# A fixed first expert for the second line of slots in a fused attention and two-layer mixture-of-experts kernel

## The chip, the cores and the metric

One core of one Trainium2 chip. The number that counts is device microseconds of one launch, the median of several runs.

## What is computed

Attention with a window (half of the heads plain, half dilated), then two mixture-of-experts layers of eight experts each. Every token goes to the one expert with the largest logit.

```python
x = attn_out.transpose(0, 2, 1, 3).reshape(2304, 512)
for layer in (1, 2):
    e_idx = argmax(x @ w_gate [+ modality_bias[modality_id] in layer 2], axis=1)
    for e in range(8):
        mask = e_idx == e
        h = maximum(x[mask] @ w1[e], 0)           # w1[e]: 512 x 1024
        out[mask] = gate[mask] * (h @ w2[e])      # w2[e]: 1024 x 512; layer 1 has one more sigmoid factor
    x = out
```

## The kernel before

The program is one long hand-ordered stream on each engine: attention (16 head pairs, function names st...), then `moe` for layer 1, then `moe` for layer 2. Instruction order on an engine is program order; a step that is to run in the middle of another one is hung on a **hook**, `(s, k)`: slot `s`, place `k` inside the slot. The tables `plan` near the end of the program (`at(s, k, ...)`) say what hangs where.

**Slots.** A slot is one block of up to 128 tokens of one expert: 96 matmuls `ph<-xT,wb` (`mm1`, two groups of 48 that fill `ph0` and `ph1`), ReLU and split of the result into a high and a low half (`hsplit`: `hh` on ScalarE, `hl` on VectorE), 24 matmuls `py<-wb` (`hh` first, then `hl`). Numbers are kept as pairs of float16 (high and low), so weights arrive as float32 in the buffer `raw` (8 pieces of 1024 columns, 512 KB each; one buffer for all experts), are rounded on ScalarE (`hi_piece`, L100, letter H in the lists) and their remainder is formed on VectorE (`lo_piece`, L105, letter L; B is both; D sends the next expert's pieces into the part of `raw` that has come free).

**Two lines of slots.** Slots 0 to 2 work on one early expert `g`, found from the first four token tiles in `first_expert`, whose weights are sent during attention. From slot 3 on, even slots walk through the first half of the list of blocks and odd slots through the second half (the list begins with expert `g` and goes round); each line has its own split weight buffer (`wb0`, `wb1`), so that one line can change its expert while the other computes. The cut is at `h`, half of the number of blocks. Which expert the odd line begins with is therefore known only after the **sort** of all tokens.

**The sort** (`sort`, a generator that runs in pieces: `run(so1)`) turns all 2304 logits into the list of token numbers of each slot. Its pieces hang at (0,0), (0,1), (0,5), (0,10), (1,3) and (2,2). The piece at (0,1) counts the blocks (`nb`, `nall`, `h`), makes the block number of each slot (`bs`, `bm`, on GpSimd, L746 to L749), then on VectorE the token positions (`ps`, `pos`, `pi`, L753 to L767) and two one-hot arrays (`ob`, `obp`, L804 and L805). The piece at (0,10) issues the gathers of tokens for slots 2 to 4, runs `table()` on VectorE (expert of each slot, where weights change) and sends slot 3's weights by that table (`start.weights(KE, always=True)`, a register loaded by SyncE from the table). The piece at (1,3) works out the gate factors on VectorE (`dl` to `gate`, L829 to L843) and GpSimd: six small operations (`gr`, `g3`, L847 to L852) and four products `Bg` (L855). The piece at (2,2) sums them on TensorE (`pg<-Bga,Aa`, L862) between the two groups of slot 2's `mm1`.

Slot 3's weights are split by `first_splits` at (1,5), (1,6), (2,0) and (2,3) of the plan (lists `FIRST`), which also sends slot 4's weights behind them. At (1,6) and (2,1) the gathered tokens of slots 2 and 3 are transposed (`x_turned`: TensorE `pxt`, then a copy on ScalarE, L901). The results of slots 0 and 1 go out at (2,5) and (2,6) (`Post1.out`, rows `y` to `y_dram`); nine spare rows of `y_dram` are filled with zeros (`zero`, on SyncE's queue).

Of the kernel before, what the change touches and what calls it, by code (L numbers as in the profile page):

```python
# [53 lines left out]
def fused(ctx, tc, qk, vw, wr1, w1a, w2a, mid, wr2, mbias, w1b, w2b, cf, c16, cbs, cms, cib, out, dbg=None):  # L54
# [646 lines left out]
    def sort(nm, lg, nt, inv, fe, ea, tab, scale, og, extra, gscale, start):  # L701
# [67 lines left out]
        def table():  # L769
# [8 lines left out]
            v.tensor_tensor(hn, nall, h, op=ALU.subtract)
            v.tensor_scalar(lim, s_odd, hn, hm, op0=ALU.mult, op1=ALU.add)
            sc = T("sc", [NSLOT])  # L780
            v.scalar_tensor_tensor(out=sc, in0=bs, scalar=-float(KA), in1=lim, op0=ALU.add, op1=ALU.min)
# [588 lines left out]
```

## Time and profile before

| what | value |
|---|---|
| median of 3 runs | 647.51 us (646.09 to 647.54) |
| the profiled execution: its own time | 648.77 us |
| its span, first to last instruction | 647.0 us |
| TensorE matmul busy | 593.6 us (92%), 7425 instructions |
| VectorE busy | 363.9 us (56%) |
| ScalarE busy | 273.0 us (42%) |
| GpSimd busy | 198.2 us (31%) |
| mean granted TensorE clock | 0.967 of full speed |

The profiled execution took 1.26 us more than the median of the runs, and 1.77 us of its time lie outside its span. Attention fills the first 152 us of the span, layer 1 goes from there to about 428 us, layer 2 to the end. Slot 0 begins at 152.3 us, slot 1 at 167.4, slot 2 at 181.1, slot 3 at 194.6, slot 4 at 209.9; later slots take 11.3 us each.

In the answers of the trace a line is: start in us, duration in us, engine, line of the program, operation, what is written and read, number of instructions merged (x), and in brackets the idle time just before and what ended it.

### The profile page before, as it was taken

The numbers are of one execution on the slowest core, as the hardware profiler recorded it, in microseconds if no ns is written. First come the engines' busy times: TensorE is split into PE (matmuls) and PEld (weight loads), VectorE is DVE, ScalarE is ACT, GpSimd is POOL, SyncE is SP. The second block draws the span as 40 slices with busy tenths as digits, with TensorE's granted clock in tenths as the row PEclk, the third lists the DMA queues.
The fourth block names the chain that finished last, engine by engine and source line by source line (L and its number), as shares of the span: only waits on it lengthen the run. The fifth ranks groups of instructions, "written<-read, shape, count | busy, mean of one in ns | idle before, by whom it ended". The sixth has DMA issues, their size and how long they took to land. (4 is left out here: it accounts for less than half of the span.)

```text
span 647.0 us, 19443 instructions
## 1 busy us (share of the span) xinstructions
PE 593.6 (92%) x7425; PEld 459.1 (71%) x7425; DVE 363.9 (56%) x643; ACT 273.0 (42%) x370; POOL 198.2 (31%) x315
## 2 busy tenths in 40 slices
PE   3989889968988999999999899989999999999994
PEld 2878778867665767777686686867686767777772
DVE  6798898898777436953848922248541111013460
ACT  5667767773184114923626511111532111114550
POOL 2567767613271310101110410001554212222220
PEclk9789989976999999999999999989999999999998
DMA  8765768972499854994877763310985534143921
GB/s 285 241 190 187 216 186 273 287 161 71 153 360 293 231 131 135 308 348 120 237 227 216 223 143 58 56 31 7 312 304 140 125 51 100 50 100 96 305 62 37
DMA packets 100865, 114.17 MB, mean 176 GB/s; under 512 B 64399, under 2 KB 69263, under 8 KB 100752
## 3 DMA queue, kind: packets, MB, share of 16 engines
q1 hardware_dynamic: 95072, 94.89, 51.3%
q0 software_dynamic: 5280, 17.13, 8.4%
q8 instruction: 60, 0.98, 0.6%
q10 hardware_dynamic: 400, 0.72, 0.3%
q14 instruction: 53, 0.43, 0.2%
HBM read 209.13 MB, written 18.22 MB: 351 GB/s over the span
## 5 line engine op out<-in xcount | busy, mean ns | idle before, releaser
L922 PEld LDWEIGHTS <-wb 128*128 128x128 f16 x4032 | 230.7, 99 | 10.1 <-issue 5.1
L922 PE MATMUL ph<-xT,wb 128*128 128x128 f16 x3648 | 211.1, 219 | 3.2 <-ACT xT L901 2.7
L933 DVE SCALAR_TENSOR_TENSOR hl<-ph,hh 128x512 f16<-128x512 f32 x84 | 57.8, 690 | 164.6 <-ACTq L941 153.5
L996 PE MATMUL py<-wb,hh 128*128 128x512 f16 x608 | 137.8, 379 | 1.7 <-ACT hh L932 1.7
L105 DVE SCALAR_TENSOR_TENSOR wb<-raw,wb 128x1024 f16<-128x1024 f32 (+1 forms) x80 | 104.9, 1350 | 16.5 <-ACT wb L100 14.3
L996 PEld LDWEIGHTS <-hh 128*128 128x128 f16 x672 | 63.6, 98 | 71.0 <-ACT hh L932 2.7
L932 ACT ACTIVATE hh<-ph 128x512 f16<-128x512 f32 x84 | 50.2, 598 | 148.9 <-PE ph L922 140.7
L100 ACT ACTIVATE wb<-raw 128x1024 f16<-128x1024 f32 (+1 forms) x80 | 87.4, 1136 | 10.5 <-DMA raw<-in_w1a 3.1
L996 PE MATMUL py<-wb,hl 128*128 128x512 f16 x304 | 71.8, 379 | 0.0
L996 PEld LDWEIGHTS <-hl 128*128 128x128 f16 x336 | 32.8, 98 | 40.0 <-DVE hl L933 0.6
L1261 POOL DMA_INDIRECT out<-y,idx x16 | 16.2, 1011 | 97.5 <-ACTq L941 78.4
L447 PE MATMUL po<-v,pT 128*96 128x65 f32 x384 | 41.6, 262 | 0.0
L447 PEld LDWEIGHTS po<-v,pT 128*96 128x96 f32 x384 | 38.4, 177 | 0.0
L386 PE MATMUL ps<-kk,qs 128*96 128x128 f16 x192 | 30.0, 229 | 4.3 <-DVE kk L344 2.2
L386 PE MATMUL ps<-kk,ql 128*96 128x128 f16 x192 | 30.1, 230 | 3.8 <-DVE ql L364 3.8
L434 ACT ACTIVATE pT<-pst 128x384 f32<-128x384 f32 x48 | 23.5, 490 | 23.0 <-PE pst L433 22.4
L387 DVE TENSOR_REDUCE M<-ps 96x4 f32<-96x512 f32 x48 | 31.6, 680 | 2.8 <-PE ps L386 2.3
L885 POOL DMA_INDIRECT xg<-x_dram,idxaa x23 | 24.4, 1063 | 27.5 <-DMA xT<-xg 15.4
L1260 ACT ACTIVATE y<-py,gsb 128x512 f32<-128x512 f32 x16 | 11.0, 687 | 51.8 <-PE py L996 51.8
L431 PE MATMUL pst<-mt,msel 128*128 128x96 bf16 x192 | 30.5, 218 | 2.4 <-ACT mt L420 2.4
L386 PEld LDWEIGHTS <-ql 128*96 128x96 f16 x192 | 23.6, 130 | 12.4 <-DVE ql L364 5.4
L433 PE MATMUL pst<-ql,kk 128*128 128x96 f16 x192 | 30.6, 219 | 0.0
(405 smaller groups left out, 730.4 us busy)
## 6 DMA issues: line engine op xcount, KB each, us to landing
raw<-in_w1a SPq DMA_DIRECT2D x95, 512.0 KB
raw<-in_w2a SPq DMA_DIRECT2D x92, 512.0 KB
raw<-in_w1b SPq DMA_DIRECT2D x75, 512.0 KB
raw<-in_w2b SPq DMA_DIRECT2D x72, 512.0 KB
qk<-in_qk SPq DMA_DIRECT2D x16, 608.0 KB
v<-in_vw SPq DMA_DIRECT2D x16, 390.0 KB
y_dram<-y SPq DMA_DIRECT2D x11, 260.0 KB
y_dram<-lotmp SPq DMA_DIRECT2D x10, 260.0 KB
```

The lines of the kernel that those rows point to most:

```text
L100: nc.scalar.activation(wb[:, 0, s], raw[:, s], AF.Copy, scale=SW)
L105: nc.vector.scalar_tensor_tensor(out=wb[:, 1, s], in0=raw[:, s], scalar=SW, in1=wb[:, 0, s], op0=ALU.mult, op1=ALU.subtract)
L386: nc.tensor.matmul(ps[:, j, :], q[:, h, QT * i:QT * i + QT], kk[:, h, QT * i:QT * i + 128], start=False, stop=w == 1 and j == 3, skip_grou ...
L387: nc.vector.tensor_reduce(out=Ms[n][:, 4 * g:4 * g + 4], in_=ps, axis=AX.X, op=ALU.max)
L431: nc.tensor.matmul(ps[:, j, :], msel[:, typ, j, :], mt[:, g, :], start=j == 0, stop=False, skip_group_check=True)
L433: nc.tensor.matmul(ps[:, j, :], kk[:, h, QT * i:QT * i + 128], q[:, h, QT * i:QT * i + QT], start=False, stop=w == 1 and j == 3, skip_grou ...
L447: nc.tensor.matmul(po[:, h, i, :], pT[:, NQ * h + i, :], v[:, h, i, :], start=True, stop=True)
L885: nc.gpsimd.indirect_dma_start(t, None, src, bass.IndirectOffsetOnAxis(start.idx[:, s:s + 1], 0))
L922: nc.tensor.matmul(ph[:, j, :], w[:, c, fs], xT[:, parts[c + i], :], start=k == 0, stop=k == 47, skip_group_check=True)
L932: nc.scalar.activation(hs, ph, AF.Relu)
L933: nc.vector.scalar_tensor_tensor(out=hl[:, 4 * g:4 * g + 4, :], in0=ph, scalar=0.0, in1=hs, op0=ALU.max, op1=ALU.subtract)
L996: nc.tensor.matmul(to, a, w, start=k == 0, stop=k == len(ops) - 1)
```

## The change

The odd line begins with the expert four places on from `g`, `(g + 4) mod 8`. `first_expert` works out that number (`gj`) and a mark of the first four experts of the list (`low`). The sort no longer cuts the list at `h` but between the fourth and the fifth expert: `a4` blocks lie before the cut, `b4` behind it; the line that runs out first takes the last blocks of the other. The weights of slot 3 are sent by `second`, in two parts, with a register loaded from `gj`: pieces 0 to 5 at (0,0), pieces 6 and 7 where the table's send was. Their split is spread over (0,5), (1,0), (1,5), (1,6), (2,0) and (2,2). Layer 2 keeps the old way.

```diff
 def slot_consts():
+        v.tensor_tensor(s_line, s_odd, s_half, op=ALU.mult)
+        v.tensor_scalar(s_line, s_line, -1.0, None, op0=ALU.add)
...
 def first_expert(nm, lg0, psum, fe):
+        if nm == "a":
+            g4, gj, low, q0 = T("g4", [P, 1]), T("gj", [P, 1], I32), T("low", [P, E]), T("q0", [P, E])
+            gp.tensor_scalar(g4, g, 4.0, -8.0, op0=ALU.is_ge, op1=ALU.mult)
+            gp.tensor_tensor(g4, g4, g, op=ALU.add)
+            gp.tensor_scalar(gj, g4, 4.0, None, op0=ALU.add)
+            gp.tensor_scalar(low, o, 4.0, None, op0=ALU.is_lt)
+            gp.tensor_scalar(q0, o, 4.0, None, op0=ALU.is_equal)
+            fe.update(gj=gj, low=low, q0=q0)
...
 def sort(...):
-        gp.tensor_scalar(bs, s_odd, h, None, op0=ALU.mult)
-        gp.tensor_tensor(bs, bs, s_half, op=ALU.add)
-        gp.tensor_scalar(bm, s_even, h, 1000.0, op0=ALU.is_ge, op1=ALU.mult)
-        gp.tensor_tensor(bm, bm, bs, op=ALU.add)
+        if start.fixed:
+            v.tensor_tensor(e8, nb, fe["low"], op=ALU.mult)
+            v.tensor_reduce(out=a4, in_=e8, axis=AX.X, op=ALU.add)
+            gp.tensor_tensor(hn, nall, h, op=ALU.subtract)
+            gp.tensor_scalar(bm, s_even, h, 1000.0, op0=ALU.is_ge, op1=ALU.mult)
+            gp.tensor_scalar(bt[:, 0], s_line, hn, 1000.0, op0=ALU.is_ge, op1=ALU.mult)
+            gp.tensor_tensor(bm, bm, bt[:, 0], op=ALU.add)
+            gp.tensor_tensor(bm, bm, s_half, op=ALU.add)
+            gp.tensor_tensor(b4, nall, a4, op=ALU.subtract)
+            v.scalar_tensor_tensor(out=bs, in0=s_odd, scalar=a4, in1=bm, op0=ALU.mult, op1=ALU.add)
+            v.tensor_scalar(bt[:, 0], s_even, a4, hn, op0=ALU.is_ge, op1=ALU.mult)
+            v.tensor_scalar(bt[:, 1], s_line, b4, hn, op0=ALU.is_ge, op1=ALU.mult)
+            v.tensor_tensor(bs, bs, bt[:, 0], op=ALU.add)
+            v.tensor_tensor(bm, bs, bt[:, 1], op=ALU.subtract)
...
         def table(...):     # three operations on VectorE become nine
...
         for i in range(KA, KA + 3):
             start.gather(i)
         table()
-        start.weights(KE, always=True)
+        if start.fixed:
+            start.second(6, 8)
+        else:
+            start.weights(KE, always=True)
...
+        def second(a, b):
+            if a == 0:
+                regs["second"] = nc.sync.value_load(fe1["gj"][0:1, 0:1], min_val=0, max_val=E - 1)
+            load_raw(w1, w2, regs["second"], pieces=range(a, b))
+            if b == 8:
+                regs.pop("second")
...
-    at(0, 0, run(so1), lambda: lo_piece(wbuf[0], 12))
+    at(0, 0, run(so1), lambda: lo_piece(wbuf[0], 12), lambda: start1.second(0, 6))
     at(0, 1, run(so1, 2))
     at(0, 2, run(fss))
-    at(0, 5, run(so1), lambda: lo_piece(wbuf[0], 14))
+    at(0, 5, run(so1), lambda: lo_piece(wbuf[0], 14), sp1("H0:4 H4:8"))
     at(0, 10, run(so1, 2))
+    at(1, 0, sp1("H8:12 L0:2"))
     at(1, 3, run(so1), start1.consts)
-    at(1, 5, lambda: start1.first_splits(FIRST[0]))
-    at(1, 6, lambda: start1.turned(KA), lambda: start1.first_splits(FIRST[1]))
-    at(2, 0, lambda: gt.memset(y16p[1][:, 2 * DM:], 0.0), lambda: start1.first_splits(FIRST[2]))
+    at(1, 5, sp1("L2:6 D0:6 H12:16"))
+    at(1, 6, lambda: start1.turned(KA), sp1("L6:10 D6:10"))
+    at(2, 0, lambda: gt.memset(y16p[1][:, 2 * DM:], 0.0), sp1("L10:12 D10:12"))
     at(2, 1, lambda: start1.turned(KA + 1))
-    at(2, 2, run(so1))
-    at(2, 3, lambda: start1.first_splits(FIRST[3]))
+    at(2, 2, run(so1), sp1("L12:16 D12:16"))
```

How this moves instructions, at the places where the order matters. TensorE's own order stays word for word the same. (Lines are those of each program; the changed one is longer, so `hl`, L933, is L976 there.)

VectorE in slot 0, behind the count of the cut (`ha`), before:

```order
L744 TENSOR_REDUCE ha<-hsa 128x1
L753 TENSOR_TENSOR e2a<-fe_Msa,nba 128x64
L754 TENSOR_REDUCE basea<-e2a 128x8
L756 SCALAR_TENSOR_TENSOR psa<-rk,basea 128x144
L757 TENSOR_TENSOR psa<-psa,oha 128x144
```

VectorE at the same place with the change:

```order
L756 TENSOR_REDUCE ha<-hsa 128x1
L760 TENSOR_TENSOR e8a<-nba,fe_lowa 128x8
L761 TENSOR_REDUCE a4a<-e8a 128x1
L768 SCALAR_TENSOR_TENSOR bsa<-slots_77,a4a,bma 128x27
L769 TENSOR_SCALAR bta<-slots_77,a4a,hna 128x27
L770 TENSOR_SCALAR bta<-slots_77,b4a,hna 128x27
L771 TENSOR_TENSOR bsa<-bsa,bta 128x27
L772 TENSOR_TENSOR bma<-bsa,bta 128x27
L781 TENSOR_TENSOR e2a<-fe_Msa,nba 128x64
L782 TENSOR_REDUCE basea<-e2a 128x8
```

Seven operations stand in front of the position arithmetic, and the third of them reads `bma`, which GpSimd writes. On GpSimd the four operations on `bs` and `bm` have become six:

```order
L762 TENSOR_TENSOR hna<-nalla,ha 128x1
L763 TENSOR_SCALAR bma<-slots_77,ha 128x27
L764 TENSOR_SCALAR bta<-slots_77,hna 128x27
L765 TENSOR_TENSOR bma<-bma,bta 128x27
L766 TENSOR_TENSOR bma<-bma,slots_77 128x27
L767 TENSOR_TENSOR b4a<-nalla,a4a 128x1
```

Behind these, `ob`, `obp`, the two `hl` of slot 0 and the array `A` follow on VectorE as before.

VectorE from the gate factors of the sort (end of slot 1) into slot 2, before:

```order
L843 RECIPROCAL gatea<-dena 128x18
L1097 SCALAR_TENSOR_TENSOR wr2h<-wr2t,wr2h 128x32
L933 SCALAR_TENSOR_TENSOR hl<-ph_3061,hh 128x512
L105 SCALAR_TENSOR_TENSOR wb_2654<-raw,wb_2654 128x2048 x3
L933 SCALAR_TENSOR_TENSOR hl<-ph_3179,hh 128x512
L105 SCALAR_TENSOR_TENSOR wb_2654<-raw,wb_2654 128x2048
L933 SCALAR_TENSOR_TENSOR hl<-ph_3296,hh 128x512
```

and with the change:

```order
L886 RECIPROCAL gatea<-dena 128x18
L1147 SCALAR_TENSOR_TENSOR wr2h<-wr2t,wr2h 128x32
L976 SCALAR_TENSOR_TENSOR hl<-ph_3097,hh 128x512
L105 SCALAR_TENSOR_TENSOR wb_2666<-raw,wb_2666 128x2048 x2
L105 SCALAR_TENSOR_TENSOR wb_2666<-raw,wb_2666 128x1024
L105 SCALAR_TENSOR_TENSOR wb_2666<-raw,wb_2666 128x2048
L976 SCALAR_TENSOR_TENSOR hl<-ph_3213,hh 128x512
L976 SCALAR_TENSOR_TENSOR hl<-ph_3329,hh 128x512
```

All remainders of slot 3's weights (a first one of 1024 columns has moved up, behind `table()`) now stand ahead of both `hl` of slot 2. On ScalarE three of the four roundings (L100, 128x2048) of these weights moved ahead of slot 1's `hh`; one is left in front of the copy of slot 2's tokens.

SyncE's queue with the change, from the last stores of attention on:

```order
L496 DMA x_dram<-x_2464 96x1x512 x6
L92 ISA
L92 DMA raw<-in_w2a 128x2x512
L92 ISA
L92 DMA raw<-in_w2a 128x2x512
L1151 DMA y_dram<-zt 128x1040 x9
L92 ISA
L92 DMA raw<-in_w2a 128x2x512
L92 ISA
L92 DMA raw<-in_w2a 128x2x512
L953 TENSOR_LOAD tab_2687
```

Pieces 0 to 3 stand ahead of these rows, around the last transposing read of attention. The nine stores of zeros stood among attention's first loads before; now they stand between pieces 5 and 6. All eight pieces now stand ahead of the load of the table's register, which stood ahead of all eight before.

## Rows read from the trace of the kernel before

**Rows 1.** The page, part 5: the group of `hl` (two in each slot).

```profile
L933 DVE SCALAR_TENSOR_TENSOR hl<-ph,hh 128x512 f16<-128x512 f32 x84 | 57.8, 690 | 164.6 <-ACTq L941 153.5
```

**Rows 2.** TensorE's waits from 170 us to the end: total us, times, longest.

```profile
PE ph L922 <- ACT xT L901: 2.7, 2, 1.6
...
PE py L996 <- ACT hh L932: 1.7, 2, 1.2
...
PE pyt L1151 <- ACT y L1132: 0.7, 1, 0.7
PE pyt L1151 <- DVE y L1133: 0.4, 1, 0.4
```

**Rows 3.** ScalarE's timeline: first rounding of slot 3's weights; `y` of slot 2.

```profile
178.19 1.91 ACT L100 ACTIVATE wb<-raw 128x2048 f16<-128x2048 f32 x1 [3.12 <-DMA raw<-in_w1a]
...
200.33 0.69 ACT L1132 ACTIVATE y<-py,gsa 128x512 f16<-128x512 f32 x1 [8.04 <-DMA y_dram<-y]
```

**Rows 4.** VectorE's timeline, the sort in slot 0.

```profile
158.17 0.18 DVE L744 TENSOR_REDUCE ha<-hsa 128x1 f32<-128x27 f32 x1
158.27 0.21 DVE L753 TENSOR_TENSOR e2a<-fe_Msa,nba 128x64 f32<-128x64 f32 x1
...
161.94 1.28 DVE L933 SCALAR_TENSOR_TENSOR hl<-ph,hh 128x512 f16<-128x512 f32 x2
```

**Rows 5.** GpSimd's timeline, the sort in slot 0; operations of this size later.

```profile
158.46 0.39 POOL L746 TENSOR_SCALAR bsa<-slots,ha 128x27 f32<-128x27 f32 x1 [4.47 <-DVE ha L744]
...
188.22 0.30 POOL L868 TENSOR_SCALAR gsa<-gsa 128x27 f32<-128x27 f32 x1
188.50 0.24 POOL L870 TENSOR_SCALAR inva<-fla 128x27 f32<-128x27 f32 x1
```

**Rows 6.** TensorE's timeline, slots 0 to 2.

```profile
162.68 1.90 PE L996 MATMUL pya<-wb,hl 128*128 128x512 f16 x8 [0.16 <-DVE hl L933]
...
181.05 1.95 PE L922 MATMUL ph<-xT,wb 128*128 128x128 f16 x32 [1.65 <-ACT xT L901]
...
184.64 1.04 PE L862 MATMUL pg<-Bga,Aa 128*128 128x108 f16 x18
```

**Rows 7.** GpSimd's timeline, the gate factors.

```profile
175.71 0.30 POOL L847 TENSOR_SCALAR gra<-gatea 128x18 f32<-128x18 f32 x1 [4.84 <-DVE wr2h L1097]
...
177.37 2.92 POOL L855 TENSOR_TENSOR Bga<-oba,g3a 128x486 f16<-128x486 f16 x3
180.24 3.05 POOL L855 TENSOR_TENSOR Bga<-oba,midf 128x486 f16<-128x486 f16 x1
```

**Rows 8.** VectorE's timeline: slot 1's first `hl`; first remainder of slot 3's weights.

```profile
172.41 0.69 DVE L933 SCALAR_TENSOR_TENSOR hl<-ph,hh 128x512 f16<-128x512 f32 x1 [1.55 <-ACT hh L932]
...
180.13 2.30 DVE L105 SCALAR_TENSOR_TENSOR wb<-raw,wb 128x2048 f16<-128x2048 f32 x1 [3.89 <-ACT wb L100]
```

**Rows 9.** GpSimd and VectorE side by side in attention.

```profile
94.15 0.77 POOL L404 CAST mb<-r 96x12 bf16<-96x12 f32 x1
95.00 0.72 POOL L405 TENSOR_TENSOR r<-r,mb 96x12 f32<-96x12 f32 x1
...
94.07 0.79 DVE L344 SCALAR_TENSOR_TENSOR kk<-qk,kk 64x608 f16<-64x608 f32 x1
94.89 0.76 DVE L364 SCALAR_TENSOR_TENSOR ql<-qk,qs 64x576 f16<-64x576 f32 x1
```

**Rows 10.** Stretches: from:to and length, PE, PEld, DVE, ACT, POOL busy, PE clock, DMA.

```profile
427.20:430.60 3.40, 1.33 (x20) 0.83 (x19) 0.92 (x2) 0.69 (x1) 0.18 (x1) 0.95 0.03 10
430.60:434.00 3.40, 3.40 (x44) 3.20 (x45) 1.97 (x6) 0.00 (x0) 1.02 (x1) 0.55 0.20 78
...
178.00:181.40 3.40, 1.75 (x14) 0.88 (x13) 1.26 (x1) 3.21 (x3) 3.40 (x4) 1.00 1.04 399
```

**Rows 11.** SyncE's queue: first weights of slot 3, first result row.

```profile
171.48 1.78 SPq L92 DMA_DIRECT2D raw<-in_w1a  x4
...
192.91 0.43 SPq L1140 DMA_DIRECT2D y_dram<-y  x1
```

More of the change, by code (lines that the diff above doesn't have):

```diff
@@ L141, in fused @@
     midf = const.tile([P, NT], F32, name="midf")
-    slots4 = const.tile([P, 4, NSLOT], F32, name="slots4")
-    s_half, s_odd, s_even, s_two = (slots4[:, i] for i in range(4))
+    slots4 = const.tile([P, 5, NSLOT], F32, name="slots4")
+    s_half, s_odd, s_even, s_two, s_line = (slots4[:, i] for i in range(5))
     lg2 = const.tile([P, NSLOT, E], F32, name="lg2")
@@ L215, in first_expert @@
         v.tensor_scalar(own, desc, m, None, op0=ALU.is_equal)
+        if nm == "a":
+            v.tensor_tensor(own, own, fe["q0"], op=ALU.add)
         yield
@@ L745, in sort @@
         bs, bm = T("bs", [NSLOT]), T("bm", [NSLOT])
[L746 to L749 removed]
+        if start.fixed:
+            a4, b4, hn, e8, bt = T("a4", [1]), T("b4", [1]), T("hn", [1]), T("e8", [E]), T("bt", [2, NSLOT])
+            v.tensor_tensor(e8, nb, fe["low"], op=ALU.mult)
[12 more added lines that the diff above has]
+        else:
+            gp.tensor_scalar(bs, s_odd, h, None, op0=ALU.mult)
+            gp.tensor_tensor(bs, bs, s_half, op=ALU.add)
+            gp.tensor_scalar(bm, s_even, h, 1000.0, op0=ALU.is_ge, op1=ALU.mult)
+            gp.tensor_tensor(bm, bm, bs, op=ALU.add)
         nbb = nb.unsqueeze(1).to_broadcast([P, E, E])
@@ L767, in sort, with table @@
         v.tensor_scalar(pi[:, 2], pi[:, 0], 127, None, op0=ALU.bitwise_and)
-        def table():
+        def table(hn=hn if start.fixed else None):
             end = T("end", [E])
@@ L775, in table @@
             v.tensor_scalar(nlast, nall, KA - 1.0, None, op0=ALU.add)
-            hm, hn, lim = T("hm", [1]), T("hn", [1]), T("lim", [NSLOT])
+            hm, lim, sc = T("hm", [1]), T("lim", [NSLOT]), T("sc", [NSLOT])
             v.tensor_scalar(hm, h, -1.0, None, op0=ALU.add)
[L778 to L781, printed above, removed]
+            if start.fixed:
+                hq = T("hq", [1])
+                v.tensor_scalar(hq, hn, -1.0, None, op0=ALU.add)
+                v.tensor_scalar(bt[:, 0], s_even, hm, None, op0=ALU.min)
+                v.tensor_scalar(bt[:, 1], s_line, hq, None, op0=ALU.min)
+                v.tensor_tensor(sc, bt[:, 0], bt[:, 1], op=ALU.add)
+                v.scalar_tensor_tensor(out=sc, in0=s_odd, scalar=a4, in1=sc, op0=ALU.mult, op1=ALU.add)
+                v.tensor_scalar(lim, bt[:, 0], a4, hn, op0=ALU.is_ge, op1=ALU.mult)
+                v.scalar_tensor_tensor(out=sc, in0=sc, scalar=1.0, in1=lim, op0=ALU.add, op1=ALU.add)
+                v.tensor_scalar(lim, bt[:, 1], b4, hn, op0=ALU.is_ge, op1=ALU.mult)
+                v.tensor_tensor(sc, sc, lim, op=ALU.subtract)
+            else:
+                hn = T("hn", [1])
+                v.tensor_tensor(hn, nall, h, op=ALU.subtract)
+                v.tensor_scalar(lim, s_odd, hn, hm, op0=ALU.mult, op1=ALU.add)
+                v.scalar_tensor_tensor(out=sc, in0=bs, scalar=-float(KA), in1=lim, op0=ALU.add, op1=ALU.min)
             cmp2 = T("cmp2", [NSLOT, E])
@@ L824, in sort @@
         table()
-        start.weights(KE, always=True)
+        if start.fixed:
+            start.second(6, 8)
+        else:
+            start.weights(KE, always=True)
         yield
@@ L1008, in slot @@
             hook(7)
-        start.part = part
+        start.part, start.second = part, second
         start.gather, start.transpose, start.turned, start.weights, start.pys = gather, x_transpose, x_turned, weights, pys
@@ L1032, in fused @@
     class Start:
-        name, next, late_low = "a", NEXT, True
+        name, next, late_low, fixed = "a", NEXT, True, True
         def hook(self, s, k):
@@ L1224, in fused @@
     class Start2(Start):
-        name, next, late_low = "b", NEXT2, False
+        name, next, late_low, fixed = "b", NEXT2, False, False
         def fields(self, g, inv, ex):
```

2 lines of the change are left out of this document (added).

## The prediction

> **What bounds the kernel now.** I began with the waits of TensorE: from 170 us to the end only a few are left, and four of them lie where the change works [rows 2]. Slot 2 starts 1.65 us late, because the copy of its tokens stands on ScalarE behind the first rounding of slot 3's weights (178.19 to 180.10 us), and that one waited 3.12 us for its transfer [rows 3, 6]. In slot 3 TensorE waits 0.7, 0.4 and 1.7 us: `y` of slot 2 could be written only at 200.33 us, after 8.04 us in which ScalarE waited for the first result row to leave the same buffer, a store issued at 192.91 us; two roundings and then `hh` stood behind it [rows 2, 3, 11]. So what the table's late send costs on TensorE's path is at most 1.6 + 2.8 = 4.4 us. Everything that the change adds to the sort must be set against that, and the next views are therefore the timelines of VectorE and GpSimd in slots 0 to 2.
>
> The amount of work stays. I put the reference's inputs through the two routers: expert 2 is `g`; 256 of its tokens go to slots 0 and 1, and the remaining blocks of experts 0 to 7 are 4, 3, 1, 3, 2, 2, 3, 3, in sum 21. That makes 23 slots, 19 follow in layer 2 with either order, and the trace has 84 `hl`, two for each of 42 slots [rows 1]. Before, the cut `h` = 11 falls just between experts 6 and 7, so that the odd line begins with 7; with the change it begins with 6, `a4` = 8, `b4` = 13, and the even line takes the last three blocks (expert 1). Both ways load eight experts. The changes of expert stay at slots 4, 10, 14 and 18 on the even line and move from 9 and 17 to 9 and 15 on the odd one; two neighbouring changes (9 and 10) went without a wait of TensorE before, so I cost this at nothing.
>
> **Term A, the sort gets longer: +2.9 us.** VectorE starts the position arithmetic at 158.27 us, right behind the count, while GpSimd works beside it [rows 4]. With the change it first makes `e8` and `a4` and then needs `bma`, the fifth of GpSimd's operations behind the count. GpSimd begins at 158.46; such operations follow each other every 0.28 us when nothing holds them up (188.22 to 188.50), the first took 0.39 [rows 5]. Five of them end at 159.8 (at 0.39 each, 160.4). Five VectorE operations of 27 columns come then, by the 0.18 to 0.21 us of the two rows at 158.17 and 158.27 plus their gaps some 0.27 each, so `e2` starts near 161.2 instead of 158.27: 2.9 us later. Lower bound: were GpSimd no part of it, seven operations of 0.21, or 1.5 us; upper bound 3.6. Nothing hides it, since both `hl` of slot 0 come behind this arithmetic on VectorE (161.94), and TensorE already waited 0.16 us for the first of them [rows 4, 6]. The table piece behind it shifts along, and gathers too.
>
> **Term B, slot 2's tokens: -1.6 us.** Three of the four roundings now run in slots 0 and 1 on transfers sent early, and the last one needs pieces sent with the sort's gathers, a slot earlier; the copy then meets no wait. Bounds: 0 and -1.65.
>
> **Term C, the gate factors: +6.8 us.** This is what I take to be decisive. `table()` is six operations longer (some 1.4 us by the same 0.2 us and gaps) and a remainder of 1024 columns (half of the 2.30 us, [rows 8]) follows it; before, VectorE had 1.55 us to spare there [rows 8], so `gate` comes about 1.0 us later against TensorE, at 176.7 instead of 175.7 [rows 7]. GpSimd then has six small operations and four products before TensorE may do `pg` at 184.64 [rows 6, 7]. Before, they fell into 3.89 us in which VectorE idled for want of rounded weights [rows 8]: three products took 2.92 us, 0.97 each, but the fourth took 3.05, and it was the one beside a remainder that ran from 180.13 to 182.43. The same shows in attention: a small GpSimd operation of 0.77 us ends at 94.92 where VectorE's two-input operation ended at 94.86, and the next takes 0.72 us to 95.72, where the next such operation ends at 95.65 [rows 9]. So beside VectorE operations that read two arrays, one GpSimd operation passes for each of them. With the change four remainders of together 8.1 us (three of 2.30, one of half) stand without a gap just behind slot 1's second `hl`. In the clock of the trace before (plus A for all): `gate` at 176.7, two small operations done by 177.35, remainders from 177.3, one small operation after each of them, the last at 185.9, then four products of 0.97: 189.8 us. TensorE, with B gained, wants `pg` at 184.64 - 1.65 = 183.0. It waits 6.8 us. Lower bound 0: if GpSimd is never held up, the products end 3.05 - 0.97 earlier than before and 1.0 later, at 182.2. Upper bound 7.5, when each small operation also delays the next remainder by its 0.2 us. I take the value near the upper end because the row nearest to it, the fourth product, shows the full wait.
>
> The Trainium skill (SBUF — State Buffer, Who interferes with whom) says that a VectorE instruction with two SBUF inputs and a GpSimd instruction that reads SBUF exclude each other for a whole instruction, and that the issue order decides who blocks. By the first half the sum is the one above; by the second, if GpSimd's operations come first each time, it would be the rival "GpSimd wins" below. The trace agrees with the first half at the 3.05 us of the fourth product.
>
> **Term D, slot 3: -2.7 us.** Slot 3's 4 MB no longer stand in the queue ahead of slot 4's weights and the first result row; before, the send began at 171.48 us and the row's buffer was free only at 200.33 [rows 3, 11]. With the change six pieces leave in the tail of attention and in slot 0, and slot 3 itself starts later by A, B and C, so the row is long gone. Bounds: 0 and -2.8.
>
> **Term E, the clock: +1.7 us.** Around 428 us TensorE is busy for 1.33 of 3.40 us, and the next 3.40 us run at 0.55 of the clock; at 178 us it is busy for 1.75 of 3.40 and the clock stays at 1.00 [rows 10]. A gap of 6.8 us is far beyond the first, so I count one such stretch, 3.4 us at half speed (1.2 instead of 2.4 GHz), 1.7 us lost. The gap of A, 3 us, may cost the same again; I keep that for the range.
>
> **At nothing:** five GpSimd operations in attention (1.4 us once, hidden behind VectorE's reduces, else +1); the nine stores of zeros, which leave a time in which no engine waited for a transfer and come to SyncE's queue ahead of pieces 6 and 7, not needed before the end of slot 1; pieces 0 to 3 beside attention's last transposing read (else +1, as its readers come soon after).
>
> **Sum:** 2.9 - 1.6 + 6.8 - 2.7 + 1.7 = +7.1 us on the profiled 648.77, so 655.9; the runs' median lies 1.26 us lower, 647.51 + 7.1 = **654.6 us**.
>
> **Rivals.**
> - *GpSimd wins.* It gets in ahead of each remainder, `pg` waits for nothing, and the remainders, late by some 5 us, are still done before slot 3. Then C is 0; with one slow stretch for A's gap: 2.9 - 1.6 - 2.7 + 1.7 = +0.3, 647.8 us. For it: products of 0.97 beside an idle VectorE. Against it: the fourth product. Chance 0.20.
> - *The early send pays* (the other side). A costs 1.5 to 2.2 us, C nothing, the clock holds: 2.2 - 1.6 - 2.7 = -2.1, 645.4 us; with A at 1.5 it is 644.7. It decides where slot 0's wait for `hl` stays under 2.4 us and `pg` does not wait. For it: both waits removed are in the rows. Against it: VectorE now waits for GpSimd in the sort. Chance 0.13.
> - *All goes wrong.* A's gap costs a second slow stretch and slot 3's waits stay: 7.1 + 1.7 + 2.7 = +11.5, 659.0 us. Chance 0.07.
> - That slot 3's weights are not early after all (pieces 6 and 7 still wait for the last remainders of expert 2, formed in slot 0) changes little: only the fourth rounding needs them. It is inside B's bounds.
>
> **How the numbers follow.** The forecast has 0.60; with the last rival 0.67 for slower by over 0.3% (1.9 us, about what a measurement of this kernel can tell from no change), 0.20 for no change, 0.13 for faster. The range leaves out the lower part of the faster case and the worst part of the last rival: 645.5 to 658.5 us.
>
> **What would show it.** TensorE's waits with the change: one of about 3 us for `hl` in slot 0; none for slot 2's tokens; a large one at `pg` for GpSimd's products, each of which starts only behind a remainder; none for `y` and `hh` in slot 3; a stretch of low clock behind the gap. If `pg` waits under 2 us, term C was wrong and with it the sign; if slot 0's wait for `hl` is under 1.5 us, term A was.

## The result and the profile after

The changed kernel took 655.08 us in the median of four runs (654.21 to 655.75), beside 647.52 us for the kernel before in the same comparison (four runs, 646.09 to 651.19): ratio 1.0107, 95% interval 1.0064 to 1.0151. It is slower; 654.6 us was predicted. The profiled execution of the changed kernel took 654.21 us with a span of 652.4 us, 5.4 us more than the span before. The profiled execution before lay 1.25 us above its median and this one 0.87 us below, so 2.1 us of the 7.6 us between the medians stand in no stretch of the table below.

Where the 5.4 us lie is read from TensorE's timeline: the start of slot 0 and the length of each slot, from the first `ph` to the next slot's first `ph`.

| stretch | before, us | after, us | difference | terms of the prediction |
|---|---|---|---|---|
| attention, to the start of slot 0 | 152.3 | 155.2 | +2.9 | "at nothing" |
| slot 0 | 15.09 | 16.91 | +1.8 | A: +2.9 |
| slot 1, with the wait for slot 2's tokens | 13.67 | 12.31 | -1.4 | B: -1.6 |
| slot 2 | 13.53 | 20.71 | +7.2 | C and E: +8.5 |
| slot 3 | 15.29 | 12.14 | -3.1 | D: -2.7 |
| slots 15 to 17 | 36.91 | 34.54 | -2.4 | "at nothing" |
| everything else | | | +0.4 | |

The waits of TensorE with the change, from 90 to 260 us (total us, times, longest):

```profile
PE pg L905 <- POOL lotmp L1254: 5.2, 1, 5.2
PE pm L430 <- POOL mb L420: 3.0, 3, 2.1
...
PE pya L1046 <- DVE hl L976: 2.2, 1, 2.2
...
PE pl L530 <- DMA xT<-x_dram: 0.9, 1, 0.9
```

The waits for `xT`, `hh` and `y` [rows 2] are gone, and in their place stand a large one at `pg` and one at `hl` of slot 0. `lotmp` is only GpSimd's last small store behind the products. The two others lie in attention: the mask `pm`, which waits for GpSimd's `mb`, and the last transposing read.

VectorE's timeline with the change, in the sort and in slot 2:

```profile
160.30 0.18 DVE L756 TENSOR_REDUCE ha<-hsa 128x1 f32<-128x27 f32 x1
...
162.22 0.25 DVE L768 SCALAR_TENSOR_TENSOR bsa<-slots,a4a,bma 128x27 f32<-128x27 f32 x1 [1.47 <-POOL bma L766]
...
163.11 0.22 DVE L781 TENSOR_TENSOR e2a<-fe_Msa,nba 128x64 f32<-128x64 f32 x1
...
166.72 1.28 DVE L976 SCALAR_TENSOR_TENSOR hl<-ph,hh 128x512 f16<-128x512 f32 x2
...
181.59 7.87 DVE L105 SCALAR_TENSOR_TENSOR wb<-raw,wb 128x2048 f16<-128x2048 f32 x4
196.04 0.69 DVE L976 SCALAR_TENSOR_TENSOR hl<-ph,hh 128x512 f16<-128x512 f32 x1 [6.59 <-ACT hh L975]
```

From `ha` to `e2` it is 2.81 us, where it was 0.10 [rows 4]: 2.7 us more, of which 1.47 us are the wait for GpSimd. The remainders stand without a gap from 181.59 to 189.46 us. GpSimd's timeline with the change, the sort (two of six operations) and the gate factors:

```profile
160.56 0.19 POOL L762 TENSOR_TENSOR hna<-nalla,ha 128x1 f32<-128x1 f32 x1 [5.73 <-DVE e8a L760]
...
161.94 0.24 POOL L766 TENSOR_TENSOR bma<-bma,slots 128x27 f32<-128x27 f32 x1
...
181.78 2.17 POOL L892 TENSOR_TENSOR gra<-gra,g3a 128x18 f32<-128x18 f32 x1
184.01 2.14 POOL L893 CAST g3a<-gra 128x18 f16<-128x18 f32 x1
186.23 1.08 POOL L894 TENSOR_TENSOR gra<-gra,g3a 128x18 f32<-128x18 f32 x1
187.38 2.14 POOL L895 CAST g3a<-gra 128x18 f16<-128x18 f32 x1
189.47 2.91 POOL L898 TENSOR_TENSOR Bga<-oba,g3a 128x486 f16<-128x486 f16 x3
192.34 1.00 POOL L898 TENSOR_TENSOR Bga<-oba,midf 128x486 f16<-128x486 f16 x1
```

Four operations of 18 columns last 2.17, 2.14, 1.08 and 2.14 us, one for each of the four remainders (the third of which has half the columns); the products start as the last remainder ends and then take 0.97 us each (2.91 for three), as before [rows 7]. TensorE's timeline with the change:

```profile
160.73 2.84 PE L965 MATMUL ph<-xsA,wb 128*128 128x128 f16 x48
...
167.46 1.90 PE L1046 MATMUL pya<-wb,hl 128*128 128x512 f16 x8 [2.16 <-DVE hl L976]
...
193.39 1.81 PE L905 MATMUL pg<-Bga,Aa 128*128 128x108 f16 x18 [5.20 <-POOL lotmp L1254]
194.99 4.05 PE L965 MATMUL ph<-xT,wb 128*128 128x128 f16 x48
```

The wait for `hl` was 0.16 us [rows 6] and is 2.16. Behind the wait of 5.20 us the same 48 matmuls take 4.05 us, 2.84 elsewhere. The clock there, in stretches of 3.4 us (span in us, TensorE busy, granted clock, DMA share, GB/s):

```profile
187.80:191.20 3.40, 0.39 (x16) 0.92 0.98 346
191.20:194.60 3.40, 1.21 (x14) 0.50 1.00 351
194.60:198.00 3.40, 3.40 (x40) 0.57 0.72 178
198.00:201.40 3.40, 3.40 (x31) 1.00 0.00 0
```

Two stretches run at 1.2 instead of 2.4 GHz. `pg` begins at 193.39 us, so most of the first is waiting anyway and costs little.

### The profile page after: what moved, and what is told of

Read it like the earlier page. It is cut to its first block, busy times and chain, and to the rows that moved or that the text cites. A ratio compares the mean times of both kernels' runs of the same rounds, so it can differ in the third digit from the quotient of the medians.

```text
span 652.4 us, 19467 instructions
## 1 busy us (share of the span) xinstructions
PE 595.5 (91%) x7425; PEld 462.1 (71%) x7425; DVE 366.1 (56%) x660; ACT 273.0 (42%) x370; POOL 205.8 (32%) x322
## 5 line engine op out<-in xcount | busy, mean ns | idle before, releaser
L976 DVE SCALAR_TENSOR_TENSOR hl<-ph,hh 128x512 f16<-128x512 f32 x84 | 57.8, 690 | 170.1 <-ACTq L991 149.5
L100 ACT ACTIVATE wb<-raw 128x1024 f16<-128x1024 f32 (+1 forms) x80 | 87.2, 1134 | 6.3 <-ACTq L991 3.8
L445 PE MATMUL pst<-qs,kk 128*128 128x96 f16 x192 | 31.2, 221 | 0.0
```

What stands on the lines that cost most here:

```text
L100: nc.scalar.activation(wb[:, 0, s], raw[:, s], AF.Copy, scale=SW)
L445: nc.tensor.matmul(ps[:, j, :], kk[:, h, QT * i:QT * i + 128], q[:, h, QT * i:QT * i + QT], start=False, stop=w == 1 and j == 3, skip_grou ...
L976: nc.vector.scalar_tensor_tensor(out=hl[:, 4 * g:4 * g + 4, :], in0=ph, scalar=0.0, in1=hs, op0=ALU.max, op1=ALU.subtract)
```

## The experiments

Each run stands with its ratio to the kernel before on the same chip (95% interval). Lengths of slots are TensorE's, as in the table above.

**1. Only the five GpSimd operations in attention, in the kernel before.**

```diff
 # before
         gp.tensor_tensor(o, o, u, op=ALU.add)
+        gp.tensor_scalar(g4, g, 4.0, -8.0, op0=ALU.is_ge, op1=ALU.mult)
...
+        gp.tensor_scalar(q0, o, 4.0, None, op0=ALU.is_equal)
```

> The kernel before, with nothing added but the five small GpSimd operations of first_expert (g4, gj, low, q0; their results are not used). Theory: the changed kernel's attention is 2.1 us late from its 98th microsecond on because these five stand on GpSimd ahead of the chain that makes mb, so that TensorE waits 2.1 instead of 0.5 us for it and its clock is halved for 3.4 us. Then this kernel is 1.6 to 2.1 us slower than before and slot 0 starts near 154.3 instead of 152.3 us. Rival: the delay comes from SyncE's early register load or from the moved stores of zeros; then this kernel is within 0.3 us of before.

649.33 us, ratio 1.0041 (1.0005 to 1.0078). Slot 0 started at 155.2 us, as with the whole change, and slots 0 to 2 kept their lengths from before. The waits of TensorE for the mask in that run, then before:

```profile
PE pm L426 <- POOL mb L416: 2.5, 2, 2.0
```

```profile
PE pm L418 <- POOL mb L408: 1.5, 3, 0.5
```

So the five operations alone make attention longer: the mask of one head pair stands behind them on GpSimd, TensorE waits 2.0 us instead of at most 0.5 (1.5 us in three waits before), and half clock follows. In all eight runs with the five operations in attention this wait is 1.8 to 2.1 us.

**2. The changed sort with the old send and the old split.** The plan of slots 0 to 2 is that of the kernel before, too.

```diff
 # changed kernel
-        if start.fixed:
-            start.second(6, 8)
-        else:
-            start.weights(KE, always=True)
+        start.weights(KE, always=True)
```

> The changed kernel's order of slots and its sort, but slot 3's weights sent by the table and split as in the kernel before. Theory: the longer sort alone costs some 2 us at slot 0's wait for hl, the five operations in attention 2 us, the wait of 1.65 us for slot 2's tokens and the 2.8 us of waits in slot 3 stay, no wait over 1 us appears at pg, and the moved change of expert on the odd line (slot 17 to slot 15) gives 2 us back, which slot 17 lost before: 1.5 to 3 us slower than before. Rival: the big wait at pg comes from the later gate factors, not from the place of the remainders: then pg waits 4 us or more here too and the kernel is 6 to 8 us slower.

651.48 us, ratio 1.0071 (1.0046 to 1.0097). GpSimd and TensorE in that run:

```profile
183.04 0.22 POOL L889 TENSOR_TENSOR gra<-gra,g3a 128x18 f32<-128x18 f32 x1
...
184.05 2.92 POOL L895 TENSOR_TENSOR Bga<-oba,g3a 128x486 f16<-128x486 f16 x3
186.93 3.05 POOL L895 TENSOR_TENSOR Bga<-oba,midf 128x486 f16<-128x486 f16 x1
```

```profile
168.68 2.62 PE L1043 MATMUL pya<-wb,hl 128*128 128x512 f16 x8 [3.32 <-DVE hl L973]
...
190.67 1.04 PE L902 MATMUL pg<-Bga,Aa 128*128 128x108 f16 x18
```

With the remainders at their old places the same small operation takes 0.22 us instead of 2.17 and `pg` waits for nothing, though the gate factors begin even later than with the whole change (182.39 against 181.13 us). TensorE too reaches `pg` later here (190.67 against 188.19 us), but that doesn't save the rival "the gate is simply late": GpSimd's chain takes 7.6 us in this run (182.39 to 189.98), and begun at 181.13 it would end 0.5 us behind 188.19, not 5.2 (an estimate from these numbers). The run cost more than expected, since here the wait for `hl` (3.32 us) was itself followed by half clock (2.62 us for eight matmuls, 1.90 otherwise). Slots 15 to 17 took 11.34, 11.62 and 11.59 us: the gain there belongs to the new cut of the list, not to the early send.

**3. The remainders behind the gate products.**

```diff
 # changed kernel
-    at(1, 5, sp1("L2:6 D0:6 H12:16"))
-    at(1, 6, lambda: start1.turned(KA), sp1("L6:10 D6:10"))
+    at(1, 5, sp1("H12:16"))
+    at(1, 6, lambda: start1.turned(KA))
...
+    at(2, 3, sp1("L2:6 D0:6"), sp1("L6:10 D6:10"), sp1("L10:12 D10:12"))
...
+    at(2, 6, first_out(post1, start1, 1), sp1("L12:16 D12:16"))
```

> The changed kernel with the remainders of slot 3's weights formed behind the first hl of slot 2 (at (2,3), the last four of 512 columns at (2,6)) instead of ahead of it, and slot 4's weights sent behind them. Theory: GpSimd's ten operations are shut out by these remainders, one passing for each; now they run beside an idle VectorE, each of the six takes 0.2 to 0.3 us instead of up to 2.17, pg waits under 1 us instead of 5.2, the 6.8 us of half clock behind it do not come, and the kernel is 5 to 7 us faster than the changed one, 0 to 2 us slower than before to 1 us faster. Rival (gate simply late): pg still waits 2 us or more and the kernel gains under 3 us.

651.26 us, ratio 1.0072 (1.0048 to 1.0096). TensorE in that run:

```profile
188.09 1.04 PE L905 MATMUL pg<-Bga,Aa 128*128 128x108 f16 x18
...
197.22 1.04 PE L1046 MATMUL py<-wb,hl 128*128 128x512 f16 x4 [1.09 <-DVE hl L976]
...
200.44 2.84 PE L965 MATMUL ph<-xT,wb 128*128 128x128 f16 x48 [1.28 <-issue]
```

The wait at `pg` and the half clock are gone (slot 2: 15.93 us), which shows the cause of term C. The span fell by only 3.3 us: `hl` of slot 2 now stands behind the remainders, and slot 4's weights, sent behind them, brought back the wait of `y` for its buffer (6.39 us on ScalarE), so that slot 3 took 13.17 us instead of 12.14.

**4. The five VectorE operations of the sort behind the position arithmetic.** They stand unchanged behind the last of the `pi`.

```diff
 # changed kernel
-            v.scalar_tensor_tensor(out=bs, in0=s_odd, scalar=a4, in1=bm, op0=ALU.mult, op1=ALU.add)
...
-            v.tensor_tensor(bm, bs, bt[:, 1], op=ALU.subtract)
...
         v.tensor_scalar(pi[:, 2], pi[:, 0], 127, None, op0=ALU.bitwise_and)
+        if start.fixed:
+            v.scalar_tensor_tensor(out=bs, in0=s_odd, scalar=a4, in1=bm, op0=ALU.mult, op1=ALU.add)
...
+            v.tensor_tensor(bm, bs, bt[:, 1], op=ALU.subtract)
```

> The changed kernel with the five VectorE operations on bs and bm moved behind the position arithmetic, so that VectorE does not wait for GpSimd's bma. Theory: the 1.47 us for which VectorE waited there go, slot 0's wait for hl falls from 2.16 to 0.5 to 1.0 us, and the kernel is 1.2 to 1.7 us faster than the changed one if nothing later takes it back; the wait at pg keeps its 5 us. Rival: the operations themselves are the cost; then the wait for hl falls by under 0.5 us.

652.35 us, ratio 1.0099 (1.0067 to 1.0131). VectorE's wait for GpSimd is gone, and `hl` starts 4.92 us behind `ha` instead of 6.42. TensorE still waited 1.93 us for it, because it too began slot 0 earlier in this run (154.2 us) while VectorE did not to the same degree. Nothing changed at `pg` (5.20 us). By the wait alone, which fell by only 0.23 us, the rival held. The expected 1.2 us are not shown, and the intervals overlap.

**5. The gate products on VectorE.**

```diff
 # changed kernel
+        q = v if start.fixed else gp
-        gp.tensor_scalar(gr[:, 0], gate, 2.0 ** 10, None, op0=ALU.mult)
+        q.tensor_scalar(gr[:, 0], gate, 2.0 ** 10, None, op0=ALU.mult)
...
-            gp.tensor_tensor(Bg[:, :, k], ob, f.unsqueeze(2).to_broadcast(sb), op=ALU.mult)
+            q.tensor_tensor(Bg[:, :, k], ob, f.unsqueeze(2).to_broadcast(sb), op=ALU.mult)
```

> The changed kernel, with layer 1's ten operations from gr to Bg on VectorE, where gate is made, instead of GpSimd; nothing else moves. Theory (term C: GpSimd is shut out by the remainders): on VectorE they take six times some 0.2 us and four times 0.67 us (as ob, of the same shape), 3.9 us, so the products are ready near 184.6 us, before TensorE wants them at 188; the wait at pg (5.2 us) and the half clock behind it (1.9 us) go, the remainders end near 193.5 us, before slot 2's hl is wanted at 195. 655.1 - 7.1 = 648.0 us; with the waits of slot 3 that came with the later remainders in the third run, up to 651. Rival (TensorE waits because the gate factors as such come late): a wait of 2 us or more at pg stays, 650 to 653 us with the half clock.

649.38 us, ratio 1.0055 (1.0034 to 1.0076). VectorE and TensorE in that run:

```profile
179.99 0.18 DVE L891 TENSOR_SCALAR gra<-gatea 128x18 f32<-128x18 f32 x1
...
181.14 1.81 DVE L899 TENSOR_TENSOR Bga<-oba,g3a 128x486 f16<-128x486 f16 x3
182.86 0.66 DVE L899 TENSOR_TENSOR Bga<-oba,midf 128x486 f16<-128x486 f16 x1
...
184.14 7.83 DVE L105 SCALAR_TENSOR_TENSOR wb<-raw,wb 128x2048 f16<-128x2048 f32 x4
```

```profile
165.59 3.52 PE L1047 MATMUL pya<-wb,hl 128*128 128x512 f16 x8 [3.43 <-DVE hl L977]
...
184.28 1.04 PE L1047 MATMUL pya<-wb,hl 128*128 128x512 f16 x4 [1.59 <-DVE hl L977]
...
188.74 1.04 PE L906 MATMUL pg<-Bga,Aa 128*128 128x108 f16 x18
```

The ten operations took 3.5 us (179.99 to 183.52) and `pg` waits for nothing; slot 2 took 13.77 us instead of 20.71, 6.9 of the 7.1 us expected. The span fell by 3.5 us. The rest was given back: `hl` of slot 1 now stands behind the products (slot 1 +1.6 us), slot 3 took 0.9 us more, and the end of layer 1 took 16.03 us instead of 14.11, on which more in runs 11 and 12. (Slot 0 began 2.6 us earlier here and took 1.7 us more.)

**6. Both `hl` of slot 0 ahead of the block numbers and one-hot arrays.**

```diff
 # changed kernel
+        if start.fixed:
+            yield
+            v.scalar_tensor_tensor(out=bs, in0=s_odd, scalar=a4, in1=bm, op0=ALU.mult, op1=ALU.add)
...
+            v.tensor_tensor(bm, bs, bt[:, 1], op=ALU.subtract)
         v.tensor_tensor(ob, bm.unsqueeze(1).to_broadcast(sb), pi[:, 1].unsqueeze(2).to_broadcast(sb), op=ALU.is_equal)
...
-    at(0, 5, run(so1), lambda: lo_piece(wbuf[0], 14), sp1("H0:4 H4:8"))
+    at(0, 5, run(so1, 2), lambda: lo_piece(wbuf[0], 14), sp1("H0:4 H4:8"))
```

> The changed kernel, with the five VectorE operations on bs and bm and the two one-hot arrays ob and obp put behind both hl of slot 0. Theory (term A: what stands ahead of hl on VectorE in slot 0 is what TensorE waits for): hl comes some 3.9 us earlier (1.47 of the wait for GpSimd, 1.05 of the five, 1.34 of the two), slot 0's wait of 2.16 us goes to 0, slot 0 is 2.0 us shorter; VectorE loses nothing since hl is ready by then, and the gather list comes no later. pg still waits, by up to 2.0 us more if the gate factors come at the same time as before: then the time stays 655, and 653 if VectorE too is ahead. Rival (VectorE has no slack behind hl): the matmul of the gather list waits for A and obp instead, slot 0 stays as long.

651.37 us, ratio 1.0103 (1.0070 to 1.0135): no gain over the changed kernel is shown. TensorE in that run:

```profile
166.05 0.39 PE L857 MATMUL pidx<-obpa,Aa 128*128 128x27 f16 x9 [1.21 <-DVE Aa L852]
167.32 0.39 PE L857 MATMUL pidx<-obpa,Aa 128*128 128x27 f16 x9 [0.88 <-DVE Aa L852]
...
190.11 1.81 PE L907 MATMUL pg<-Bga,Aa 128*128 128x108 f16 x18 [4.88 <-POOL lotmp L1256]
```

The wait for `hl` is gone, and 2.09 us of waiting for `A` stand in its place, as the rival said: in slot 0 of this run TensorE waits for VectorE's last piece, whichever that is.

**7. The five GpSimd operations moved from attention to the start of slot 0.**

```diff
 # changed kernel, first_expert
+        def marks():
+            g4, gj, low, q0 = T("g4", [P, 1]), T("gj", [P, 1], I32), T("low", [P, E]), T("q0", [P, E])
+            gp.tensor_scalar(g4, g, 4.0, -8.0, op0=ALU.is_ge, op1=ALU.mult)
...
+            gp.tensor_tensor(own, own, q0, op=ALU.add)
+        fe.update(marks=marks)
...
-    at(0, 0, run(so1), lambda: lo_piece(wbuf[0], 12), lambda: start1.second(0, 6))
+    at(0, 0, lambda: fe1["marks"](), run(so1), lambda: lo_piece(wbuf[0], 12), lambda: start1.second(0, 6))
```

> The changed kernel, with the five GpSimd operations of the first expert (and the sum on own) moved out of attention to the start of slot 0, so that SyncE loads the register there and pieces 0 to 3 leave behind attention's last stores. Theory: attention's mask wait and the half clock behind it go (2.1 us by the first run's difference, 1.8), and the last transposing read has the queue alone (0.9 us); slot 0 starts at 152.3 instead of 155.2 us. 655.1 - 2.9 = 652.2 us. ScalarE needs piece 0 in slot 0's second half, some 6 us after the send: if it comes late, slot 0's remainders and roundings shift, at most the 1.6 us of slot 2's tokens come back, 653.8 us. Rival: the clock and not the five operations made attention longer, then slot 0 starts at 154 or later.

651.87 us, ratio 1.0095 (1.0074 to 1.0115). Slot 0 began at 152.1 us, as expected, and `pm` and the transposing read waited as in the kernel before. But slot 0 took 18.53 us: TensorE, now earlier, waited 3.5 us for `hl`, with half clock behind it. Of 3.1 us won in attention 1.6 were lost there. Over all runs, slot 0 began at 152.6 to 155.6 us with the five operations in attention (eight runs, the changed kernel and run 12 among them) and at 151.5 to 152.4 without (the kernel before and five runs).

**8. All three edits (5, 6 and 7) together.**

> All three edits together: products on VectorE, hl first, marks late. Theory (the terms are separate places): 655.1 - 7.1 - 2.0 - 2.9 = 643.1 us, 0.7% under the kernel before; what the change really gains, slot 2's tokens 1.65, slot 3's waits 3.1 and the switch of slot 17, 2.0, is left over, less the longer VectorE work. Rival (a gain in one place turns into a wait at the next, as with the late remainders): 646 to 649 us, with waits in slots 2 and 3 for y, hh or the gather list.

646.67 us, ratio 1.0001 (0.9982 to 1.0021): the loss is gone, a gain isn't there, as the rival said. Slots 0 to 3 took 16.20, 14.08, 13.96 and 12.79 us, in sum 57.0 (57.6 before; 62.1 with the change). TensorE's waits there were the 2.2 us for `A`, then 1.6 us for `hl` and 1.1 for `hh` of slot 1. The end of layer 1 again took 15.80 us.

**9. The gate factors behind both `hl` of slot 1.**

```diff
 # run 8
-    at(1, 3, run(so1), start1.consts)
-    at(1, 5, sp1("L2:6 D0:6 H12:16"))
+    at(1, 5, run(so1), start1.consts, sp1("L2:6 D0:6 H12:16"))
```

> The run with all three edits, and the gate factors moved from the middle of slot 1 to its end, behind both hl. There TensorE still waited 1.15 us for hh and 1.60 us for hl of slot 1, both of which stood behind the gate factors. Theory: these 2.75 us go, and since the products come at the same time on VectorE (near 181.5 us) TensorE now waits 0 to 1 us at pg: 646.7 - 2.2 = 644.5 us. Rival (VectorE is full in slots 0 to 2, so that a wait only moves): 2 us or more at pg or for slot 2's hl, 646 to 647 us.

647.02 us, ratio 0.9996 (0.9977 to 1.0015). The waits for `hl` and `hh` of slot 1 are gone, and a new one of 2.03 us stands before slot 2, for its tokens: the wait only moved, though not to one of the places that the rival named.

**10. The gather list's matmul later as well.** The last remainder of expert 2 now also stands ahead of `A`.

```diff
 # run 9
-    at(0, 5, run(so1, 2), lambda: lo_piece(wbuf[0], 14), sp1("H0:4 H4:8"))
-    at(0, 10, run(so1, 2))
-    at(1, 0, sp1("H8:12 L0:2"))
+    at(0, 5, run(so1), lambda: lo_piece(wbuf[0], 14), run(so1), sp1("H0:4 H4:8"))
+    at(1, 0, sp1("H8:12"))
+    at(1, 1, run(so1, 2), sp1("L0:2"))
```

> The run before this one, and in slot 0 the last remainder of expert 2 (1.2 us) ahead of the array A, and the gather list's matmul a third of a slot later, in slot 1. With all three edits TensorE waited 2.2 us for A and 0.3 us for that remainder at the end of slot 0. Theory: these 2.5 us go, the gathers come at most 1 us later: 644.5 - 2 = 642.5 us. Rival (VectorE is full): slot 0 is 2.5 us shorter, and slots 1 and 2 longer by as much.

648.03 us, ratio 1.0011 (0.9992 to 1.0029). Slot 0 took 13.79 us, slot 1 16.12: the rival held again. ScalarE and TensorE in that run:

```profile
179.06 1.91 ACT L100 ACTIVATE wb<-raw 128x2048 f16<-128x2048 f32 x1 [1.70 <-DMA raw<-in_w2a]
180.87 0.99 ACT L948 COPY xT<-pxt 128x1024 f16<-128x1024 f16 x1
```

```profile
181.92 3.32 PE L969 MATMUL ph<-xT,wb 128*128 128x128 f16 x32 [2.99 <-ACT xT L948]
```

That is the wait of [rows 3, 6] once more: the copy of slot 2's tokens behind a rounding that waits for its transfer, here that of pieces 6 and 7. Term B gained only as long as TensorE was late for other reasons.

**11. Run 10 with 16 small stores more on VectorE in slot 12.**

```diff
 # run 10
+    def padding():
+        for _ in range(16):
+            vt.memset(pad, 0.0)
+    at(12, 7, padding)
```

> The run before this one, and 16 stores of 128x1 zeros on VectorE in slot 12, where it idles. In the two runs with the gate products on VectorE the last y of layer 1 started 2.96 us after VectorE's previous work with no releaser shown, where it takes 1.44 behind ScalarE otherwise, and TensorE lost 1.5 us and another 3.4 us of half clock there. Theory: that is where VectorE's own stream of instructions is cut (it has ten more in front), so that a shift by 16 changes it: the wait is 0.4 us again and the time 2 to 3 us lower than without. Rival (it has another cause, such as the timing of layer 1): the same 1.9 us wait.

**12. The changed kernel with ten such stores.**

> The changed kernel, and ten stores of 128x1 zeros on VectorE in slot 12, so that as many instructions stand ahead of layer 1's end as with the gate products on VectorE; nothing else. Theory (the place in VectorE's stream decides): the last y of layer 1 comes 1.5 us late here too, layer 2 starts 1.5 us later, and the half clock behind it may double: 656.6 to 658.3 us against 655.1, all else as in the changed kernel. Rival: no difference, 655.1.

Run 11: 645.82 us, ratio 0.9983 (0.9965 to 1.0001), the lowest of all. Run 12: 656.24 us, ratio 1.0125 (1.0084 to 1.0165), beside 1.0107 for the changed kernel; the intervals overlap, so here the rows show the loss, not the time. VectorE's last `y` of layer 1, in run 11, then in the changed kernel, then in run 12:

```profile
425.93 0.75 DVE L1183 SCALAR_TENSOR_TENSOR y<-py,prg,y 128x512 f16<-128x512 f32 x1 [1.44 <-ACT y L1182]
```

```profile
434.80 0.75 DVE L1179 SCALAR_TENSOR_TENSOR y<-py,prg,y 128x512 f16<-128x512 f32 x1 [1.44 <-ACT y L1178]
```

```profile
437.01 0.75 DVE L1179 SCALAR_TENSOR_TENSOR y<-py,prg,y 128x512 f16<-128x512 f32 x1 [3.03 <-issue]
```

Ten more VectorE instructions, by the gate products or in slot 12, make this `y` start some 3 us behind VectorE's work before it with no releaser shown, and 16 on top take that away again. The last slot of layer 1 took 15.87 us in run 12 and 14.12 in run 11. So runs 5 and 8 to 10, which have nine or ten instructions more by the gate products, lost 1.7 to 1.9 us there to the place that this instruction has in VectorE's stream. Run 11 lies 2.2 us below run 10 in the median (645.82 against 648.03). Not all of that is the earlier `y`: in run 10 the granted clock was 0.50 from 428.0 to 434.8 us, in run 11 it stayed at 1.00 there, and the first slot of layer 2 took 13.54 and 11.56 us. In the changed kernel, without the late `y`, one such stretch at 0.51 follows and that slot takes 12.87 us; why run 11 has none no run shows. And run 11's interval against the kernel before still touches 1: that it beats that kernel is likely, not shown.

## Why the prediction was right

The sign and the size came out (+7.1 us forecast; +5.4 between the profiled executions, +7.6 between the medians), by the mechanism named as decisive. The terms were less good than their sum: slots 0 to 3, where all five of them lie, lost 4.5 us instead of 7.1, and the rest, put at nothing, added 0.9. That the median came within 0.5 us of the forecast is partly luck, since it includes the 2.1 us that no stretch shows.

- **Term C, the gate factors, +6.8 forecast, 5.2 measured.** Shown by runs 2, 3 and 5, which take the wait away in three ways: remainders in their old places, remainders later, products off GpSimd. The step "one small operation after each of them" came out: each ends within 0.1 us of a remainder's end. (The paragraph "What would show it" says of the products that each starts behind a remainder; they follow all four, as the sum has it.) The chain from GpSimd's first operation on `gate` to the last product took 12.2 us (181.13 to 193.34) where the sum had 13.1; the other 0.8 us are TensorE's, which reached `pg` 7.1 us behind that first operation (188.19) instead of 6.3.
- **Term E, the clock, +1.7 forecast, 2.0 measured** (1.81 - 1.04 of `pg` and 4.05 - 2.84 of the 48 matmuls behind it). It was two stretches of 3.4 us, not one, but some 2.7 of the 6.8 us were waiting (by the granted clock it fell near 190.7 us, and `pg` began at 193.39).
- **Term A, the sort, +2.9 forecast.** VectorE's part was right (2.7 us later at `e2`, with 1.47 us for GpSimd). TensorE lost 2.0: the step "nothing hides it" left out that TensorE might start slot 0 later too. `ha` came 5.1 us behind the start of slot 0 (160.30 - 155.2), 5.9 before (158.17 - 152.3), so VectorE was 0.8 us further ahead. Run 12, the same code up to slot 12, shows the other side: slot 0 began 1.3 us earlier (153.9), the wait for `hl` was 3.42 us with half clock behind it, and slot 1 began 0.5 us later. How the loss divides between attention and slot 0 thus differs from one execution to the next.
- **Term B, -1.6 forecast, -1.4 measured; term D, -2.7 forecast, -3.1 measured.** The new rows on ScalarE show both: the copy of slot 2's tokens has no wait, and `y` of slot 2 no longer waits for a buffer.

```profile
182.19 1.00 ACT L944 COPY xT<-pxt 128x1024 f16<-128x1024 f16 x1
...
204.73 0.69 ACT L1182 ACTIVATE y<-py,gsa 128x512 f16<-128x512 f32 x1 [2.01 <-PE pyt L1201]
```

- **"At nothing": two misses that cancel.** The first is "five GpSimd operations in attention (1.4 us once, hidden behind VectorE's reduces, else +1)". They are not hidden. Two of the five were themselves shut out by VectorE's two-input operations, as [rows 9] could have told:

```profile
94.16 0.64 POOL L213 TENSOR_TENSOR fe_g4a<-fe_g4a,fe_ga 128x1 f32<-128x1 f32 x1
94.89 0.74 POOL L214 TENSOR_SCALAR fe_gja<-fe_g4a 128x1 int32<-128x1 f32 x1
```

  With the half clock behind the mask wait and the 0.9 us of the last transposing read (the other "else +1"), slot 0 began 2.9 us late. Run 1 shows the five operations' wait, but not their share of the 2.9: there the clock stood at 0.50 for two stretches behind the mask wait, not one, and no wait for the transposing read came up. The second miss is the move of a change of expert from slot 17 to 15. I took its cost as nothing from the pair 9 and 10. The pair 17 and 18 was not like it, as this row of the kernel before shows, which I had not looked for; behind six remainders in a row (6.90 us on VectorE), TensorE waited for `lg`, the logits of layer 2's router:

```profile
362.57 0.44 PE L1160 MATMUL plg<-wr2h,yT 128*128 128x8 f16 x12 [1.84 <-DVE lg L1169]
```

  With the change slot 17 takes 11.59 instead of 13.59 us, in run 2 too, where the old send stays.
- **The rivals.** "GpSimd wins" is out: GpSimd came second at every remainder. The Trainium skill (SBUF — State Buffer, Who interferes with whom) has the two engines exclude each other for a whole instruction, and the trace agrees at 2.17 us for an operation of 0.22. Its other half is that the issue order decides who blocks. Run 2 agrees from GpSimd's side; there VectorE came second:

```profile
186.17 2.95 DVE L105 SCALAR_TENSOR_TENSOR wb<-raw,wb 128x2048 f16<-128x2048 f32 x1 [3.24 <-ACT wb L100]
```

  This remainder began 0.8 us before GpSimd's third product ended (186.97) and took 2.95 us, where the next takes 2.29; the fourth product, second in its turn, took 3.05. So GpSimd can win, but only where it is there first, which it was at none of the four remainders of the changed kernel. "The early send pays" failed at its own condition, a wait for `hl` under 2.4 us and none at `pg`: the first held (2.16), the second not. Run 8, where `pg` does not wait, reaches 646.67, not 645.4.

**What stays open.** Whether a version clearly beats the kernel before: run 11 leaves 3 us of waiting for slot 2's tokens, and sending pieces 6 and 7 earlier wasn't tried. Also how much of attention's length is the five operations and how much the clock, which falls at other places there in each run (slot 0 began anywhere from 152.6 to 155.6 us with the five operations ahead of it).

## What to carry to other kernels

Before a stream of two-input operations is moved on VectorE, list every chain of small operations on GpSimd that runs beside it: here each link beside them cost one whole VectorE operation (2.17 us for 0.22), and moving the chain to VectorE (3.5 us here) can be cheaper than leaving it. Where one engine is full over several stages, a wait taken away on another shows up at the next thing it needs: runs 6, 9 and 10 each removed 2 to 3 us of waiting, and none shows a gain. A sum that comes out right is no proof of its terms; here +2.9 and -2.4 us that had been put at nothing cancelled.
